# An attention and token-MLP block on one core: single-bank accumulator tiles, first norm transposed by DMA, three levels in the first MLP

## The chip, the cores and the metric

The kernel runs on one core of one Trainium2 chip. The metric is the device time of one execution in microseconds (us). The kernel before took 238.85 us (median of 4 runs made beside the changed kernel, 238.24 to 239.48). A ratio below is always the mean time of one kernel's fast runs over that of the other's fast runs of the same rounds on the same chip, so it is not quite the ratio of the medians that stand beside it. The medians and ranges of the experiments are over all runs. The span of a profiled execution, from first to last instruction, is about 2 us shorter than its time.

Engines are named as in the profile: PE is TensorE (matmuls), PEld its weight loads, DVE is VectorE, ACT is ScalarE, POOL is GpSimd, SP is SyncE, whose queue issues the DMAs.

## The reference, cut to what matters

```python
# S = 2048 tokens, D = 512, H = 32 heads of 16, window of 8 keys at distance 0, 2, ..., 14; F = 1792
x = A_x
sa, ca, ga, sb, cb, gb = the six rows of silu(c) @ w_mod          # "mod rows"
h = layernorm(x) * (1 + ca) + sa                                  # first norm
q, k, v = h @ wqkv
o = softmax over the 8 keys (q . k / 4, keys before the start masked) applied to v
x = x + ga * (o @ wo)
h = layernorm(x) * (1 + cb) + sb                                  # second norm
u = gelu(layernorm(h) mixed over TOKENS by w1 (S x F) + b1)       # third norm, first MLP
x = x + gb * (u mixed back over tokens by w2 (F x S) + b2)        # second MLP
```

Tokens are worked in 16 tiles of 128, grouped in five chunks of 2, 4, 4, 4 and 2 tiles. The attention of one chunk is: norm, transpose, QKV matmuls, products of query and key on VectorE (summed over a head by TensorE), softmax, products of weight and value on VectorE (summed by TensorE), output projection. The value products need shifted copies of v, called vD, which DMAs make inside the on-chip memory, 16 a chunk. The first MLP sums over all 2048 tokens, so it can begin on the tiles that are done and end only with the last one.

## The kernel before, cut to what the change touches

The program is a graph of operations with estimated durations. A small list scheduler in the kernel decides each engine's order of instructions once, from those estimates and from priorities; on the chip the order of each engine is fixed. Any change of a duration, a priority or a buffer count can therefore move instructions far away.

```python
psG = [psp.tile([P, 1024], F32, name=f"psG{i}") for i in range(3)]     # three accumulator tiles of two banks
def ps(slot):
    lo = slot.i % 2 * 512
    return psG[slot.i // 2][:, lo:lo + slot.size * 512]                # a slot is one bank or a pair
PR = dict(tr=1, qkv=2, a2=2, o=2, wo=2, mlp=2)                         # how many banks a group takes
w_raw_t = T([P, KT * 3 * D], BF, "w_raw")                              # q, k and v weights in one tile
# ... [cut]
# first norm of a chunk -> n_sb (one buffer); 16 transposes a chunk of four tiles on TensorE into an
# accumulator; scaled by (1 + ca), sa on the way out
for k2 in range(KG):
    for sl in tiles:
        nc.tensor.transpose(trp[:, ...], n_sb[:, sl, (k0 + k2) * P:(k0 + k2 + 1) * P], ident[:])
# ... [cut]
# first MLP in four levels of tiles: 0-5, 6-9, 10-13, 14-15. At the end of a level the partial sums are
# parked in gT (bf16); the next level carries them in again by a matmul with the identity.
LEVELS=(2, 3, 4)
nc.tensor.matmul(bank(), lhsT=ident[:], rhs=gT[:, ft, :], start=True, stop=False)   # carry-in, 14 a level
```

## Time and profile before

| | before |
|---|---|
| time, median | 238.85 us |
| span of the profiled run | 236.5 us |
| TensorE busy | 206.4 us (87%) |
| VectorE busy | 157.8 us (67%) |
| chunk 0's QKV begins | 10.55 us |
| chunk 1's QKV begins | 33.90 us |

First part of the page (busy us, share of the span, instructions), before:

```profile
PE 206.4 (87%) x1413; PEld 100.6 (43%) x1436; DVE 157.8 (67%) x231; ACT 129.4 (55%) x209; POOL 3.7 (2%) x29
```

Second part of the page, before: the span in 40 slices of 5.9 us, busy tenths of TensorE and its granted clock in tenths of full speed.

```profile
PE   0493678899988995889999999999999999999992
...
PEclk9999599999999999999999999999999999999998
```

TensorE is the fullest engine and is full from the middle on. Its idle time lies at the start and around the fifth to the eighteenth slice, where it works beside a nearly full VectorE. In the fifth slice the clock is halved too. In the first slices the clock row is no measure: it shows 9 there, yet equal groups of matmuls ran at very different speed (the timeline below); the trace's record of the clock begins only with its first change (at 16.7 us here).

The costliest groups of the page, before (busy us, mean ns of one, then the idle time before them and what ended it):

```profile
L188 PE MATMUL psG_63<-hT_71,w_raw 128*128 128x256 bf16 (+1 forms) x62 | 13.0, 360 | 3.3 <-DMA w_raw<-in_A_wqkv_dram 3.2
...
L188 DVE TENSOR_TENSOR big_78<-q_sb_72,k_c_74 128x2048 bf16<-128x2048 bf16 (+1 forms) x5 | 8.2, 1646 | 8.9 <-issue 8.9
```

Chunk 0's QKV waited 3.2 us for weights, and VectorE stood 8.9 us before its first query-key product.

The timeline of TensorE, before (start, duration, what; in brackets the wait before it):

```profile
10.55 0.37 PE L188 MATMUL psG_63<-hT_71,w_raw 128*128 128x256 bf16 x1 [2.20 <-DMA w_raw<-in_A_wqkv_dram]
11.96 3.39 PE L188 MATMUL psG_63<-hT_71,w_raw 128*128 128x256 bf16 x15 [1.04 <-DMA w_raw<-in_A_wqkv_dram]
15.14 2.67 PE L188 MATMUL psG_61<-hT_71,w_raw 128*128 128x256 bf16 x16
17.65 1.91 PE L188 MATMUL psG_62<-hT_71,w_raw 128*128 128x256 bf16 x16
...
33.90 1.89 PE L188 MATMUL psG_61<-hT_71,w_raw 128*128 128x512 bf16 x8 [0.49 <-DVE ga_bc L188]
```

Equal groups of 16 matmuls take 3.4, 2.7 and 1.9 us. The table of stretches, before (start:end, length, then busy us and instructions of each engine, granted clock, DMA share, GB/s):

```profile
40.00:60.00 20.00, 19.00 (x146) 9.00 (x147) 18.69 (x23) 13.45 (x22) 0.00 (x0) 1.00 0.65 141
60.00:80.00 20.00, 17.67 (x157) 8.31 (x159) 19.81 (x18) 17.63 (x27) 0.00 (x0) 1.00 0.83 118
80.00:100.00 20.00, 17.12 (x130) 9.53 (x131) 18.36 (x26) 16.09 (x32) 0.00 (x0) 1.00 0.35 63
100.00:120.00 20.00, 18.58 (x184) 8.91 (x186) 17.69 (x13) 14.16 (x23) 0.00 (x0) 1.00 0.75 164
...
33.90:232.30 198.40, 189.08 (x1273) 88.78 (x1294) 139.70 (x190) 115.21 (x185) 0.00 (x0) 1.00 0.53 124
```

The first column after the length is TensorE. From chunk 1's QKV to the last matmul it is busy 189.1 us of 198.4, so idle 9.3.

### The profile page before, as it was taken

How to read it: one execution, taken by the hardware profiler on the slowest of the kernel's cores; microseconds unless marked ns; L12 is line 12 of the kernel's file. 1: busy time of each engine (PE TensorE's matmuls, PEld its weight loads, DVE VectorE, ACT ScalarE, POOL GpSimd, SP SyncE). 2: the span in 40 equal slices, each digit the busy share in tenths (PEclk: the TensorE clock that was granted, in tenths of full speed). 3: DMA queues.
4: the chain of work that ended last, by engine and by line, in shares of the span. 5: the costliest groups of instructions: out<-in, count | busy, mean ns of one | idle time of the engine just before them, and what ended most of it. 6: DMA issues, size and time to landing. Idle time of an engine off the chain costs nothing.

```text
span 236.5 us, 3678 instructions
## 1 busy us (share of the span) xinstructions
PE 206.4 (87%) x1413; PEld 100.6 (43%) x1436; DVE 157.8 (67%) x231; ACT 129.4 (55%) x209; POOL 3.7 (2%) x29
## 2 busy tenths in 40 slices
PE   0493678899988995889999999999999999999992
PEld 0372434444443343653433334434444444444451
DVE  4207979997999979989969987662600044444445
ACT  3324649567997699695578688755769300000000
POOL 6000000000000000000000000000000000000000
PEclk9999599999999999999999999999999999999998
DMA  6999634359919930339954810479795511111411
GB/s 198 353 304 309 139 114 147 118 180 158 157 31 154 155 45 0 93 117 223 186 139 123 237 46 8 127 227 264 229 251 141 155 47 44 44 44 47 122 44 46
DMA packets 42565, 32.92 MB, mean 139 GB/s; under 512 B 4020, under 2 KB 42292, under 8 KB 42548
## 3 DMA queue, kind: packets, MB, share of 16 engines
q1 hardware_dynamic: 42540, 32.69, 56.1%
q8 instruction: 11, 0.18, 0.4%
q14 instruction: 6, 0.05, 0.1%
q10 hardware_dynamic: 8, 0.00, 0.0%
HBM read 22.03 MB, written 2.10 MB: 102 GB/s over the span
## 4 chain that ended last, share of the span: by engine, by line
PE 58%; DVE 17%; ACT 11%; issue 7%; DMA 4%; SPq 1%; DVEq 0%; ACTq 0%
PE psG_61 L188 21%; PE psG_62 L188 21%; PE psG_63 L188 15%; ACT xx L188 3%; DMA w_raw<-in_A_wqkv_dram 3%; DVE big_78 L188 2%; DVE big_79 L188 2%; DVE st_0_1_123 L188 2%; DVE big_80 L188 2%; ACT junk L188 2%; ACT h_69 L188 2%; PE psL L188 1%; DMA vD_93<-v_c_77 1%; SPq L188 1%; DVE st_2_1_143 L188 1%
## 5 line engine op out<-in xcount | busy, mean ns | idle before, releaser
L188 PEld LDWEIGHTS <-w_raw 128*128 128x128 bf16 x282 | 30.8, 114 | 28.1 <-issue 7.6
L188 DVE SCALAR_TENSOR_TENSOR o_sb_95<-psG_62,b2col,gb_bc 128x512 f32<-128x512 f32 x6 | 4.5, 748 | 24.6 <-PE psG_62 L188 24.6
L188 PEld LDWEIGHTS <-wst_99 128*128 128x128 bf16 x128 | 12.2, 98 | 15.6 <-issue 1.8
L188 PE MATMUL psG_61<-hT_71,w_raw 128*128 128x512 bf16 (+1 forms) x78 | 17.8, 372 | 0.9 <-DVE ga_bc L188 0.5
L188 PE MATMUL psG_62<-hT_71,w_raw 128*128 128x256 bf16 (+1 forms) x95 | 17.7, 327 | 0.5 <-ACT hT_71 L188 0.4
L188 PEld LDWEIGHTS <-wst_100 128*128 128x128 bf16 x128 | 12.4, 98 | 12.6 <-issue 0.8
L188 PE MATMUL psG_63<-hT_71,w_raw 128*128 128x256 bf16 (+1 forms) x62 | 13.0, 360 | 3.3 <-DMA w_raw<-in_A_wqkv_dram 3.2
L188 DVE TENSOR_TENSOR big_78<-q_sb_72,k_c_74 128x2048 bf16<-128x2048 bf16 (+1 forms) x5 | 8.2, 1646 | 8.9 <-issue 8.9
L188 PEld LDWEIGHTS <-ident 128*128 128x128 bf16 (+1 forms) x99 | 7.9, 97 | 12.4 <-issue 5.6
L188 PEld LDWEIGHTS <-wst_98 128*128 128x128 bf16 x80 | 7.5, 98 | 10.7 <-issue 2.9
L188 DVE TENSOR_TENSOR n_sb<-o_sb_95,xx 128x512 bf16<-128x512 f32 (+1 forms) x17 | 11.2, 660 | 0.6
L188 PE MATMUL psG_62<-h_69,wst_99 128*128 128x512 bf16 x40 | 10.8, 379 | 0.5 <-issue 0.3
L188 ACT ACTIVATE gT<-psG_62 128x1024 bf16<-128x1024 f32 x9 | 9.2, 1017 | 3.4 <-PE psG_62 L188 3.4
L188 PE MATMUL psG_63<-h_69,wst_99 128*128 128x512 bf16 x39 | 10.7, 380 | 0.1
L188 DVE SCALAR_TENSOR_TENSOR o_sb_95<-psG_61,b2col,gb_bc 128x512 f32<-128x512 f32 (+1 forms) x6 | 4.2, 703 | 8.0 <-PE psG_61 L188 8.0
L188 PEld LDWEIGHTS <-o_sb_95 128*128 128x128 bf16 x64 | 6.0, 98 | 7.9 <-issue 0.8
L188 DVE TENSOR_TENSOR big_80<-q_sb_73,k_c_75 128x4096 bf16<-128x4096 bf16 x4 | 9.1, 2282 | 0.0
L188 PE MATMUL psG_62<-h_69,wst_100 128*128 128x512 bf16 x35 | 8.9, 380 | 0.1
L188 ACT ACTIVATE gT<-psG_63 128x1024 bf16<-128x1024 f32 x7 | 7.1, 1016 | 2.7 <-PE psG_63 L188 2.7
L188 DVE BATCH_NORM_STATS2 st_1_0_132<-xx 128x6 f32<-128x512 bf16 x6 | 4.1, 675 | 6.6 <-ACT xx L188 6.6
L188 DVE SCALAR_TENSOR_TENSOR o_sb_95<-psG_63,b2col,gb_bc 128x512 f32<-128x512 f32 (+1 forms) x5 | 3.5, 693 | 6.3 <-PE psG_63 L188 6.3
L188 PEld LDWEIGHTS <-group_102 128*32 128x32 bf16 x128 | 2.7, 95 | 11.3 <-issue 10.5
(211 smaller groups left out, 427.8 us busy)
## 6 DMA issues: line engine op xcount, KB each, us to landing
wst_99<-in_B_w_dram SPq DMA_DIRECT2D x3, 768.0 KB, 5.2
wst_100<-in_B_w_dram SPq DMA_DIRECT2D x3, 768.0 KB, 4.7
out_dram<-n_sb SPq DMA_DIRECT2D x15, 128.0 KB, 1.7
wst_99<-in_B_w_dram SPq DMA_DIRECT2D x2, 896.0 KB, 4.9
w_raw<-in_A_wqkv_dram SPq DMA_DIRECT2D x3, 512.0 KB, 7.1
xx<-in_A_x_dram SPq DMA_DIRECT2D x3, 512.0 KB, 9.2
w_raw<-in_B_w_dram SPq DMA_DIRECT2D x1, 1344.0 KB, 8.1
vD_93<-v_c_77 SPq DMA_DIRECT2D x8, 130.0 KB, 3.6
```

The source lines that it names most:

```text
L188: r = fn(*a, **k)
```

## The change

The intent: take work from TensorE (fewer carry-ins, transposes done by DMA), start earlier (loads in the order in which they are needed, weights in three tiles so that nothing waits for all of them, warm-up matmuls), and let evictions and matmuls interleave more finely (one-bank tiles). The second norm's sums of nine tiles come from ScalarE's accumulated output; before it was six. The scheduler's priorities were tuned anew.

```diff
-    LEVELS=(2, 3, 4),
+    BOUNDS=(6, 10),            # three levels: tiles 0-5, 6-9, 10-15
+    NPRE=5,                    # five groups of the last level start before its last tiles are there
-    NHT: int = 1,
+    NHT: int = 2,
-    LN2A=(0, 2, 2, 2, 0),
+    POOLN1=(3, 5, 7, 8, 11),   # first norm of five tiles on GpSimd
+    LN2D=(2, 3, 10, 11, 12, 14, 15),   # second norm's sums on VectorE; the others on ScalarE
+    XDMA=(1, 2, 3, 4),         # chunks whose transposes are DMAs
...
-    psG = [psp.tile([P, 1024], F32, name=f"psG{i}") for i in range(3)]
+    psS = [psp.tile([P, 512], F32, name=f"psS{i}") for i in range(6)]
-    w_raw_t = T([P, KT * 3 * D], BF, "w_raw")
+    w_r = ring(3, [P, KT, D], BF, "w_qkv")
...
+    def f_warm():
+        for i in range(36):
+            nc.tensor.matmul(ps(s_w)[:, 0:P], lhsT=ident[:], rhs=ident[:], start=True, stop=True)
...
+    dma(rowA, wmod_view[:, :, 3 * D:6 * D], 3 * D * D * 2, [], ["rowA"], "ld_wmod345")   # 1.5 MB in one load
...
+        if ch in XDMA:
+            for sl, st in enumerate(tiles):
+                nc.sync.dma_start_transpose(out=hT[:, :, sl * P:(sl + 1) * P], in_=h3[:, st, :])
+            # then hT is scaled in place on ScalarE or VectorE
...
+RANK = {'st1': -69.27, 'ln1': -327.95, 'tr': -152.8, ...}     # priorities, tuned
+BIAS = {'n1': 1.63, 'hT': 2.81, 'ev': 1.88, ...}
```

Cut: the rewriting of the norms' helper functions for one tile at a time, the homes of the second MLP's weights, four output buffers instead of two. The first norm is now computed ahead into the buffer h3, where the third norm's results go later.

## The prediction

> **What bounds it now.** The span is 236.5 us (median time 238.9). Busy times: TensorE 206.4, VectorE 157.8, ScalarE 129.4. In the table of stretches TensorE is 87% full, and its idle time lies in three places: before 10.5 us (loads, first norm), 18–54 us (8.8 us idle; 6.8 us of it also at a granted clock of 0.5), 54–120 us (6.6 us idle). After 120 us it is idle under 1 us until 230.7; then 5.8 us of tail. So: start-up latency, then TensorE and VectorE coupled, then TensorE alone.
>
> In the timeline, chunk 0's first query-key product starts at 18.96 (VectorE idle 8.9 us): its 48 QKV matmuls start at 10.55, stall for a weight load and run slowly (first group 3.4, last 1.9). Chunk 1's QKV starts at 33.9.
>
> **What the change does to TensorE.**
> - Levels of the first MLP go from four to three: 14 carry-in matmuls fewer, at 0.216 us each (from the timeline: 1.29 per six): −3.0 us.
> - 56 of 64 transposes go to DMA: the transposes hold 6.0 us, so −5.0 us.
> - 36 dummy matmuls before the first load lands take the slow clock away from chunk 0's QKV: about −2.3 us. The Trainium skill ("TensorE: Matmul & The Clock Gate", Part 1) has the array at half clock until busy for some 3.4 us; the 3.4/2.7/1.9 us of equal QKV groups agree.
>
> **Start-up.** Weights in three tiles and the first query/key groups evicted by half banks let the first product start at about 13.5 instead of 19 (estimate: start 10.5, 32 matmuls of 256 columns at 0.11 us, partly). But the order puts chunk 1's hT scaling behind chunk 0's a2 eviction on ScalarE, and about 6 MB of loads stand before the first transposes in the queue (about 18 us at the 350 GB/s of the 6–12 us stretch). Estimate for chunk 1's QKV: about 28.5 instead of 33.9.
>
> **What stays.** VectorE's work hardly changes: counting its instructions with the trace's durations gives the same total (nine parks of 0.68 us come, norms leave). ScalarE rises by about 6 us (512-wide evictions at 0.58 against 1.02 for 1024). Five norms go to GpSimd, hidden.
>
> **Sum.** TensorE: 196.8 from 33.9 to 230.7, minus 8.5 idle, 3.0 carry-ins, 3.6 transposes, 2 mod rows: 179.5. 28.5 + 179.5 + 5.8 tail = 214 without idle. VectorE: 118 us of work after 24.5 us, thus last h3 at 142 without gaps; after it 73 matmuls (15.8), the second MLP (48.4) and the tail: 212. Both are nearly full, in fixed order, so I add 6 us of mutual waits: span about 219.
>
> **Predicted: 221 us**, range 214 to 229. Faster by over 2%: 0.95; within 2%: 0.04; slower: 0.01.
>
> **What would show it.** First query-key product at 13–15 us, chunk 1's QKV at 27–30, no slow clock in chunk 0's QKV; TensorE busy about 195; VectorE's busy time within 3 us of before, last h3 at 146–151; TensorE full from there; tail unchanged near 5.8 us.
>
> **What would make it wrong.** The trace has no DMA transposes. The skill ("DMA: Bandwidth & Descriptors", Latency and other measured facts) gives 261 GB/s for them, an estimated 0.5 us for 128 KB; if each takes several us or holds the queue in front of the vD copies, chunks 2 to 4 wait and TensorE idles (230 or more). A slow-clock stretch at 18–25 us may stay. If the order fits the chip better, waits fall to 2 us: 215.

## The result, and the profile after

| | before | after |
|---|---|---|
| time, median (lowest to highest) | 238.85 us (238.24 to 239.48) | 227.82 us (226.77 to 228.17) |
| ratio of fast runs (95% interval) | | 0.9529 (0.9497 to 0.9561) |
| span of the profiled run | 236.5 us | 225.9 us |
| first query-key product | 18.96 us | 15.33 us |
| chunk 1's QKV begins | 33.90 us | 35.54 us |
| from there to the end of the span | 202.6 us | 190.4 us |

The kernel became 4.7% faster. The last two rows say where: chunk 1's QKV begins 1.6 us later, and 12.2 us were won after it. The mark is not quite like for like. In the kernel before, two of the four mod rows, the end of chunk 0's softmax and its value sums come after chunk 1's QKV has begun; in the changed kernel all mod rows, the softmax and two of the four value sums come before it.

First and second part of the page, after (slices of 5.6 us):

```profile
PE 205.7 (91%) x1380; PEld 98.5 (44%) x1402; DVE 157.9 (70%) x236; ACT 131.2 (58%) x279; POOL 11.6 (5%) x35
...
PE   7596647879999999989999999999999999999993
...
PEclk9769885999999999999999999999999999999999
```

VectorE's busy time did not change (157.8 and 157.9). The dip of TensorE in the sixteenth slice (5 tenths before) is gone. The clock row is low in more of the first slices than before; since the row is no measure in the first slices (above), this does not show that TensorE was slower there than before.

The costliest groups of the page, after:

```profile
L191 PE MATMUL psS<-hT,w_qkv 128*128 128x512 bf16 (+1 forms) x235 | 50.2, 363 | 1.3 <-ACT hT L191 0.7
...
L191 DVE TENSOR_TENSOR big<-a2sb,vD 128x4096 bf16<-128x4096 bf16 (+1 forms) x20 | 36.9, 1860 | 6.9 <-DMA vD<-v_c 6.7
```

The QKV matmuls do not wait for weights any more. VectorE now waits 6.7 us for the vD copies.

The timeline of TensorE, after:

```profile
9.22 8.95 PE L191 MATMUL psS<-hT,w_qkv 128*128 128x256 bf16 x48 [0.65 <-ACT hT L191]
...
24.85 1.04 PE L191 MATMUL psS<-gT,sc_rep 128*128 128x512 bf16 x4 [0.95 <-DMA gT<-in_w_mod_dram]
25.72 0.40 PE L191 MATMUL psS<-lsb,ident 128*128 128x64 bf16 x8
25.95 3.57 PE L191 MATMUL psS<-gT,sc_rep 128*128 128x512 bf16 x8
...
29.59 0.42 PE L191 MATMUL psS<-lsb,selA 128*32 128x64 bf16 x32
32.80 0.62 PE L191 MATMUL psS<-big,stack 128*32 128x256 bf16 x8 [2.79 <-DVE big L191]
34.99 0.62 PE L191 MATMUL psS<-big,stack 128*32 128x256 bf16 x8 [1.57 <-DVE big L191]
35.54 1.90 PE L191 MATMUL psS<-hT,w_qkv 128*128 128x512 bf16 x4
```

In TensorE's order the mod rows' matmuls (`gT,sc_rep`), chunk 0's softmax (`lsb`) and two of its value sums (`big,stack`) all stand before chunk 1's QKV, the last line. What comes before them waits for a 1.5 MB load and for VectorE.

On ScalarE, after, the scaling of chunk 1's transposed input stands behind the eviction of chunk 0's softmax weights:

```profile
30.76 0.58 ACT L191 ACTIVATE a2sb<-psS 128x512 bf16<-128x512 f32 x1
...
32.41 2.93 ACT L191 ACTIVATE hT<-hT,sacol,a1col 128x512 bf16<-128x512 bf16 x4
```

The queue that issues the DMAs, after (timeline of SyncE):

```profile
21.59 5.13 SPq L191 DMA_DIRECT2D vD<-v_c  x6
26.82 3.86 SPq L191 DMA_TRANSPOSE hT<-h  x3
30.72 2.56 SPq L191 DMA_DIRECT2D vD<-v_c  x4
33.40 1.21 SPq L191 DMA_TRANSPOSE hT<-h  x1
34.65 4.09 SPq L191 DMA_DIRECT2D vD<-v_c  x5
38.84 3.85 SPq L191 DMA_TRANSPOSE hT<-h  x3
42.74 0.61 SPq L191 DMA_DIRECT2D vD<-v_c  x1
```

The queue is occupied almost without a gap from 21.6 to 42.7 us. In these lines one transpose of 128 KB holds it for 1.2 to 1.3 us, and a vD copy for 0.6 to 0.9 on average. The copies of chunk 0 and the transposes of chunks 1 and 2 take turns. The last copy of chunk 0 is issued at 42.74, behind three transposes of chunk 2. VectorE's last value product of chunk 0 waits for it, and TensorE's fourth value sum for that product (timelines of VectorE and of TensorE, after):

```profile
45.06 1.23 DVE L191 TENSOR_TENSOR big<-a2sb,vD 128x2048 bf16<-128x2048 bf16 x1 [2.49 <-DMA vD<-v_c]
```

```profile
46.34 0.40 PE L191 MATMUL psS<-big,stack 128*32 128x256 bf16 x8 [1.94 <-DVE big L191]
```

The table of stretches, after:

```profile
8.90:15.70 6.80, 6.23 (x28) 4.10 (x29) 3.52 (x9) 3.27 (x7) 0.00 (x0) 0.50 1.11 344
...
40.00:60.00 20.00, 17.85 (x120) 8.10 (x121) 16.60 (x14) 15.03 (x28) 0.00 (x0) 1.00 0.82 201
60.00:80.00 20.00, 19.39 (x189) 8.75 (x190) 19.15 (x16) 18.25 (x42) 0.00 (x0) 1.00 0.87 129
80.00:100.00 20.00, 18.95 (x139) 9.19 (x140) 19.07 (x23) 19.39 (x46) 0.00 (x0) 1.00 0.96 148
100.00:120.00 20.00, 19.84 (x157) 9.45 (x157) 19.66 (x29) 18.10 (x43) 0.00 (x0) 1.00 1.13 189
...
35.54:222.51 186.97, 182.26 (x1168) 83.54 (x1185) 134.54 (x185) 111.14 (x239) 0.00 (x0) 0.99 0.65 140
```

From chunk 1's QKV to the last matmul TensorE is busy 182.3 us (before 189.1) and idle 4.7 (before 9.3). So of the 11.4 us won there 6.8 are busy time and 4.6 are waits; the tail after the last matmul gives the other 0.8. The 6.8 us are not all removed work: two mod rows only moved in front of the mark, and from 35.5 to 39.6 us the changed kernel runs at half clock, where the kernel before did not. The largest wait that remains is between 40 and 60 us, 2.15 us, of which 1.94 is the wait just shown.

### The profile page after: what moved, and what is told of

Read it like the earlier page. It is cut to its first block, busy times and chain, and to the rows that moved or that the text cites. A ratio compares the mean times of both kernels' runs of the same rounds, so it can differ in the third digit from the quotient of the medians.

```text
span 225.9 us, 3720 instructions
## 1 busy us (share of the span) xinstructions
PE 205.7 (91%) x1380; PEld 98.5 (44%) x1402; DVE 157.9 (70%) x236; ACT 131.2 (58%) x279; POOL 11.6 (5%) x35
## 4 chain that ended last, share of the span: by engine, by line
PE 61%; DMA 12%; SPq 9%; ACT 8%; DVE 6%; issue 3%; DVEq 0%; ACTq 0%
PE psS L191 58%; SPq L191 9%; DMA gT<-in_w_mod_dram 5%; DVE big L191 5%; DMA vD<-v_c 5%; PE psL L191 2%; ACT hT L191 2%; DMA hT<-h 2%; ACT h L191 2%; ACT xx L191 1%; ACT junk L191 1%; ACT v_c L191 1%; ACT a2sb L191 1%; DVE m L191 1%; DVE st L191 1%
## 5 line engine op out<-in xcount | busy, mean ns | idle before, releaser
L191 PE MATMUL psS<-h,wst 128*128 128x512 bf16 x216 | 53.2, 379 | 0.4
L191 PE MATMUL psS<-hT,w_qkv 128*128 128x512 bf16 (+1 forms) x235 | 50.2, 363 | 1.3 <-ACT hT L191 0.7
L191 PEld LDWEIGHTS <-wst 128*128 128x128 bf16 x308 | 29.7, 98 | 33.1 <-issue 1.5
L191 PEld LDWEIGHTS <-w_qkv 128*128 128x128 bf16 x282 | 31.1, 116 | 27.8 <-issue 9.3
L191 DVE TENSOR_TENSOR big<-a2sb,vD 128x4096 bf16<-128x4096 bf16 (+1 forms) x20 | 36.9, 1860 | 6.9 <-DMA vD<-v_c 6.7
L191 DVE SCALAR_TENSOR_TENSOR h<-psS,bcol,gb_bc 128x512 f32<-128x512 f32 (+1 forms) x17 | 12.2, 719 | 41.3 <-PE psS L191 41.3
L191 DVE TENSOR_TENSOR big<-q_sb,k_c 128x4096 bf16<-128x4096 bf16 (+1 forms) x20 | 36.8, 1857 | 0.5 <-PE psL L191 0.5
L191 DVE BATCH_NORM_STATS2 st<-xx 128x6 f32<-128x512 bf16 x23 | 15.6, 677 | 7.9 <-DMA xx<-in_A_x_dram 7.2
L191 ACT ACTIVATE h<-xx,nb,rs 128x512 bf16<-128x512 bf16 x26 | 19.9, 804 | 0.2 <-DVE nb L191 0.2
L191 PE MATMUL psS<-gT,big 128*128 128x512 bf16 x82 | 18.2, 379 | 0.1
L191 PE MATMUL psS<-woq,o_sb 128*128 128x512 bf16 x60 | 16.3, 380 | 1.2 <-ACT o_sb L191 0.9
L191 PEld LDWEIGHTS <-big 128*128 128x128 bf16 x116 | 9.2, 97 | 11.4 <-DMA big<-in_w_mod_dram 1.2
```

What stands on the lines that cost most here:

```text
L191: r = fn(*a, **k)
```

## The experiments

Twelve kernels ran, each with five rounds beside the kernel before. The changed kernel is 0.9529, or 227.82 us, in the same measure. The questions were: which part of the change brings the gain after 35 us, and why did the start-up bring none? Where an expectation names a theory by a letter, C is the clock (TensorE too slow at the start), D the one-bank tiles as the source of the gain, and E the 1.5 MB load of the mod rows. Some edits leave the order of instructions as it was; others make the scheduler find a new order, and then the order is a second change. Each paragraph says which. Running the kernels' scheduler again confirms it: it gives the same list of operations wherever the text says "same order". It also corrects a name. What the expectations of the two runs with copies on GpSimd call the start of chunk 2's QKV (46.7 us) is the group after chunk 0's last value sum; by that list it is chunk 1's last query-key group, and chunk 2's QKV begins at 53.00 us.

### Transposes back on TensorE, for all chunks (new order)

```diff
-        ...prompt_kernel(tc, *args)
+        ...prompt_kernel(tc, *args, XDMA=())
```

> All 64 transposes go back to TensorE, everything else of the change kept (the scheduler orders anew). Theory A (the DMA transposes buy TensorE time, as predicted): TensorE's transposes come back, 56 x 0.09 us, and the time rises by about 5 us, to 233. Theory B (in the start-up they cost on the one DMA-issuing queue, 1.3 us of issue each, what they save on TensorE): chunk 1's QKV starts earlier than 35.5 us (30 to 32) and the total stays within 2 us of 227.8.

Measured: 230.33 us, ratio 0.9645 (0.9614 to 0.9676). In this new order the DMA transposes are worth about 2.5 us net (2.8 by the ratios), half of the 5.0 us of TensorE work that they remove by my estimate. The start differs more than the total. Timeline of TensorE in this kernel:

```profile
24.48 1.02 PE L191 MATMUL psS<-hT,w_qkv 128*128 128x512 bf16 x4
...
30.20 1.92 PE L191 MATMUL psS<-hT,w_qkv 128*128 128x512 bf16 x7
```

Chunk 1's QKV begins 11 us earlier, though only with its first four matmuls (the next begin at 30.20, in the changed kernel at 37.66), and the kernel is still slower. An early start of chunk 1 is not worth its own length when the order later loses it.

### Transposes back on TensorE for chunk 1 alone (new order)

```diff
+        ...prompt_kernel(tc, *args, XDMA=(2, 3, 4))
```

> Only chunk 1's four transposes go back to TensorE, which is idle at that time anyway; chunks 2 to 4 stay on DMA. Theory B: the vD copies of chunk 0 no longer stand behind 5 us of transpose issues, chunk 1's QKV starts at 30 to 32 instead of 35.5, total about 224. Theory A (start-up bound by the 1.5 MB modulation load and the slow clock, not by the issue queue): QKV start within 1 us of 35.5, total within 1.5 us of 227.8.

Measured: 229.27 us (227.44 to 233.82; two of the six runs slow), ratio 0.9576 (0.9547 to 0.9606). By the ratios that is 1.1 us slower than the changed kernel, but the intervals overlap, so it is not clear of noise; it is not faster, though chunk 1's QKV begins at 24.3 us (again with four matmuls; the next at 29.4). Here too the gain at the start was lost in the new order: between 60 and 120 us, most of it from 80 to 100, where TensorE is busy 15.28 us instead of 18.95. This miss shows that the start of chunk 1 alone does not set the total.

### Plain copies in place of the transposes (same order, result wrong)

```diff
-  nc.sync.dma_start_transpose(out=hT[:, :, sl * P:(sl + 1) * P], in_=h3[:, st, :])
+  nc.sync.dma_start(hT[:, :, sl * P:(sl + 1) * P], h3[:, st, :].rearrange("p (k n) -> p k n", k=KT))
```

> Every DMA transpose is replaced by a plain DMA copy of the same 128 KB from the same tile to the same place, in exactly the same order (wrong result on purpose). Theory B (issue cost of transposes on the queue delays the vD copies and hT): issues fall from 1.3 to about 0.5 us each, 14 x 0.8 = 11 us of queue time goes, of which the 8 in the first 45 us count: chunk 1's QKV starts at 31 to 33, total 224 to 225. Theory A: the time stays within 1 us.

Measured: 224.38 us (222.62 to 224.84), ratio 0.9374 (0.9345 to 0.9403); relative error 0.021, wrong. So with the same bytes, order and buffers, the kind of the DMA costs 3.4 us. From issue to landing the two kinds hardly differ (median of the eight up to 43 us: 2.6 us for a transpose, 2.4 for a copy). The timeline of SyncE in this kernel shows what differs:

```profile
26.17 2.00 SPq L191 DMA_DIRECT2D hT<-h  x3
...
35.15 2.76 SPq L191 DMA_DIRECT2D hT<-h  x3
```

Three issues take 2.00 and 2.76 us instead of 3.86 and 3.85. Chunk 0's last value sum no longer waits, and chunk 1's last query-key group begins at 44.18 us instead of 46.67 (chunk 2's QKV at 50.51 instead of 53.00). Chunk 1's QKV begins at 34.82 instead of 35.54. That is no more than between runs: with one warm-up matmul and the old queue (below) it is 34.81. So the queue is not what holds that one.

### Four levels in the first MLP again (new order)

```diff
+        ...prompt_kernel(tc, *args, BOUNDS=(6, 10, 14))
```

> First MLP in four levels as before (14 carry-in matmuls more, 14 parks more), the rest of the change kept, order scheduled anew. If TensorE bounds the second half one to one, 14 x 0.216 = 3.0 us more, 230 to 231. Rival: VectorE and ScalarE waits hide it, or the earlier start of level 10-14 gives it back: within 1 us.

Measured: 230.16 us (229.84 to 230.51), ratio 0.9635 (0.9615 to 0.9654). The 14 carry-ins are worth 2.3 us (2.5 by the ratios); I had 3.0 (14 times 0.216). The new order is TensorE's old one for its first 199 of 248 operations, so little else changed.

### One warm-up matmul instead of 36 (same order)

```diff
-        for i in range(36):
+        for i in range(1):
```

> 35 of the 36 dummy matmuls are taken away, all else in the same order. After's trace shows the granted clock full from 5.5 to 8.9 us, when TensorE only waits, and half from 8.9 to 15.7, when chunk 0's QKV runs (48 matmuls in 8.95 us, 7.6 before the change). Theory C (the dummies end too early, so they buy nothing): time within 1 us of 227.8, QKV block again 7.5 to 9 us. Rival, the prediction's: without them QKV is slower still and the total rises by about 2 us.

Measured: 228.44 us (226.29 to 230.27; three of the six runs slow, the fast ones 226.29 to 227.19), ratio 0.9499 (0.9461 to 0.9537): no difference clear of noise. Chunk 0's 48 QKV matmuls begin at 10.1 us and take 7.8, instead of 9.2 and 8.95, so they end at about the same time. TensorE is busy 3.6 us less, which answers one wrong point of the prediction: these matmuls count as busy time and do nothing else.

### Dummy matmuls in more of the gaps (same order)

```diff
+    def spin(slot, n):
+        for _ in range(n):
+            nc.tensor.matmul(ps(slot)[:, 0:P], lhsT=ident[:], rhs=ident[:], start=True, stop=True)
+    # 24 before the mod columns, 12 before chunk 0's transposes, 16 before its QKV,
+    # 14 and 24 before two of the mod rows, 44 before chunk 0's first value sum
```

> Dummy matmuls are put also into the idle gaps that follow (before the two modulation-column groups, before chunk 0's transposes and QKV, before two modulation rows, before chunk 0's first value product), all else in the same order. Theory C (slow clock at 9-16, 26-29 and 33-40 us is a real cost of the start-up): chunk 0's QKV takes 5.5 to 6 us instead of 8.95, no half clock before 40 us, total 222 to 225. Rival (start-up bound by loads, the issue queue and VectorE, TensorE's speed does not matter there): within 1 us of 227.8.

Measured: 232.0 us (229.95 to 233.74; one of the six runs slow), ratio 0.9698 (0.9655 to 0.974), 4 us slower. The clock was what I wanted in chunk 0's QKV. Timeline of TensorE in this kernel:

```profile
11.94 5.07 PE L191 MATMUL psS<-hT,w_qkv 128*128 128x256 bf16 x45 [0.19 <-ACT hT L191]
...
37.19 5.31 PE L191 MATMUL psS<-hT,w_qkv 128*128 128x512 bf16 x12
```

Chunk 0's QKV ran at full speed, 45 matmuls in 5.07 us, and chunk 1's began 1.7 us later than without the dummies. So a full clock in chunk 0's QKV alone does not bring an earlier start, and theory C's 222 to 225 us did not come. That the clock costs nothing is not shown: the run does not separate what the dummies themselves delay, and the issuing queue was slower in it too (the six vD copies took 6.05 us instead of 5.13, the three transposes after them 5.00 instead of 3.86), so that chunk 0's second value product waited 2.59 us for its copies instead of 0.89.

### The vD copies of chunks 0 and 1 issued by GpSimd (same order)

```diff
-        return add("sp", 0.6, lambda: nc.sync.dma_start(...
+        return add("sp", 0.6, lambda: getattr(nc, q).dma_start(...       # q="sync" unless given
-        f"vd{ch}_{dhi}{w4}", rate=150e3, ...)
+        f"vd{ch}_{dhi}{w4}", rate=150e3, q="gpsimd" if ch < 2 else "sync", ...)
```

> The 32 vD copies of chunks 0 and 1 are issued by GpSimd, which is nearly idle, instead of the queue that issues the transposes; order otherwise the same. Theory B (queue time of transposes and vD copies, one behind the other, holds chunk 0's value products and chunk 2's hT): vD waits of VectorE fall from 6.7 us to under 2, chunk 2's QKV starts 2 us or more before 46.7, total 224 to 225, as with plain copies. Rival: GpSimd's issue is as slow, or the landing and not the issue counts: within 1 us, or slower.

Measured: 229.45 us (228.05 to 232.8; one of the six runs slow), ratio 0.9604 (0.9551 to 0.9657), slower than the changed kernel by 1.6 us, just about clear of noise (the intervals touch). Chunk 1's last query-key group did begin 3.2 us earlier (43.51). It was lost between 60 and 80 us: chunk 1's copies landed after 8.1 us, ScalarE waited 4.9 us for transposes, and TensorE was busy 8.0 of the 10 us from 60 to 70.

### Only chunk 0's 16 vD copies issued by GpSimd (same order)

The same edit with `ch < 1`.

> Only chunk 0's 16 vD copies are issued by GpSimd; in vd_pool chunk 2's QKV began at 43.5 instead of 46.7 us, but chunk 1's copies, issued there too, then collided with chunk 3's transposes (8.1 us to land, ScalarE waited 4.9 us for hT). Theory B: the start-up gain of about 3 us stays now, total 224 to 226. Rival: the gain is given back anyway because VectorE and ScalarE set the pace after 50 us: within 1 us of 227.8.

Measured: 225.0 us (223.8 to 228.03; one of the six runs slow), ratio 0.9388 (0.9356 to 0.9419), and the result is correct. It beats both kernels: 2.8 us below the changed one, and 6.1% below the kernel before. The table of stretches of this kernel:

```profile
40.00:60.00 20.00, 20.00 (x128) 8.62 (x126) 17.43 (x14) 15.76 (x31) 0.00 (x0) 0.95 0.87 185
60.00:80.00 20.00, 19.79 (x198) 8.61 (x197) 19.03 (x19) 18.74 (x42) 0.00 (x0) 1.00 0.85 134
```

TensorE's remaining wait between 40 and 60 us is gone (20.00 busy instead of 17.85, a little of it at half clock). The DMAs did not land sooner after their issue: the vD copies took 6.6 us (median) instead of 3.1, the transposes up to 43 us 8.8 instead of 2.6. Together with the plain copies this shows that the occupied issuing queue cost the changed kernel about 3 us there. The Trainium skill ("DMA: Bandwidth & Descriptors", Rules for kernel authors) says of spreading DMAs over several engines that it does not help bandwidth, "it only saves sequencer issue time". Issue time was what was short, and 16 issues moved away brought 2.8 us. Chunk 1's QKV still began at 34.75 us.

### The six one-bank tiles declared as three two-bank tiles (same order)

```diff
-    psS = [psp.tile([P, 512], F32, name=f"psS{i}") for i in range(6)]
+    psG = [psp.tile([P, 1024], F32, name=f"psG{i}") for i in range(3)]
-        return psS[slot.i][:]
+        return psG[slot.i // 2][:, slot.i % 2 * 512:slot.i % 2 * 512 + 512]
```

> The six single-bank PSUM tiles are declared as three tiles of two banks again, still used bank by bank, in the same order; the built program then waits on later events of the neighbour bank. Theory D (single-bank tiles pay by finer waits): 2 to 5 us slower, as TensorE waits for evictions of the bank beside. Rival: the waits were slack anyway: within 1 us.

Measured: 240.2 us (239.01 to 240.81), ratio 1.0046 (1.0013 to 1.008). The same instructions in the same order, on the same bytes, are 12.4 us slower than the changed kernel: the whole gain and a little more. Only the declaration changed, so only the waits that are derived from it can differ. Two views of this kernel, first the table of stretches:

```profile
160.00:180.00 20.00, 18.45 (x85) 8.20 (x84) 5.38 (x12) 9.94 (x16) 0.00 (x0) 1.00 0.40 112
```

and the timeline of TensorE:

```profile
168.94 1.03 PE L191 MATMUL psG<-h,wst 128*128 128x512 bf16 x4
170.75 0.59 PE L191 MATMUL psG<-h,wst 128*128 128x512 bf16 x2 [0.78 <-ACT gT L191]
```

In the last level of the first MLP, where the changed kernel is busy 19.89 of 20 us, TensorE stops in the middle of a group of six matmuls, in a bank that it is already filling, until ScalarE has emptied another one. That this is the other bank of the pair is inferred from the declaration; the trace does not name the bank. This stretch shows 1.4 of the 12.4 us; most other stretches between 20 and 200 us lose 0.7 to 2.2 us each. The Trainium skill ("PSUM — Partial Sum Buffer", PSUM bank collisions raise a hardware error) gives the bank as the unit to guard: "Semaphore-guard PSUM by bank × quadrant (by bank is the simple version), not by address." A two-bank tile is guarded more coarsely than that. No run here shows a collision; what this one shows is the price of the coarser guard.

### The kernel before with six one-bank tiles (new order)

```diff
-    PR = dict(tr=1, qkv=2, a2=2, o=2, wo=2, mlp=2)
+    PR = dict(tr=1, qkv=1, a2=1, o=1, wo=1, mlp=1)
-    psG = [psp.tile([P, 1024], F32, name=f"psG{i}") for i in range(3)]
+    psS = [psp.tile([P, 512], F32, name=f"psS{i}") for i in range(6)]
```

> The kernel before, with one part of the change alone: six single-bank PSUM tiles in place of three two-bank tiles, so all evictions become one bank wide (the scheduler orders anew). Undoing that declaration in the changed kernel cost 12.4 us, more than the whole gain. Theory D (the two-bank tile couples neighbours, and freeing them is the main source of the gain, in whatever order): before gains 3 us or more, 236 or less. Rival D2 (the kernel before already claims and frees both banks of a pair together, so it suffered little from it; the 12 us are what the new order would lose without single-bank tiles): within 2 us of 238.8, or slower because 1024-wide evictions (1.02 us) become two of 0.58.

Measured: 237.82 us (236.38 to 238.94), ratio 0.9951 (0.9917 to 0.9984). Alone, one-bank tiles bring 1.2 us. The two runs belong together: the tiles are needed for the new order to work, and alone they do not bring the gain. One limit remains: the priorities were not tuned again for this kernel, so what a tuned order would make of the tiles alone is not shown.

### The mod-row load put later (new order)

```diff
-    dma(rowA, wmod_view[:, :, 3 * D:6 * D], ...)                        # among the first loads
+    dma(rowA, wmod_view[:, :, 3 * D:6 * D], ..., after=last vD of chunk 0)
```

The twelve matmuls of these rows and the first MLP's first weight loads moved behind it.

> The 1.5 MB load of three modulation rows, their 12 matmuls and the first MLP weight loads go behind chunk 0's vD copies; rows are needed only from about 70 us (scheduler orders anew; vD copies stay on the old queue). Theory E (chunk 0's softmax stood behind those matmuls on TensorE, from 24.0 to 29.5 us): first value product before 29 instead of 31.5 us, chunk 1's QKV at 31 to 33 instead of 35.5, total 224 to 226. Rival: the queue of DMA issues holds chunk 1's QKV at 35 anyway: within 1 us of 227.8.

Measured: 232.74 us (232.33 to 233.86), ratio 0.9745 (0.9716 to 0.9773), 5 us slower. Chunk 1's QKV begins at 33.78, only 1.8 us earlier, and chunk 2's is then 0.8 us later than in the changed kernel (53.84 instead of 53.00). Later, between 100 and 120 us, TensorE loses time (busy 17.71 us instead of 19.84). In this order theory E explains 1.8 us; what the load costs in the old order was not tried.

### The second norm's sums of all tiles on VectorE (new order)

```diff
+        ...prompt_kernel(tc, *args, LN2D=tuple(range(16)))
```

> The changed kernel with the second norm's sums of all tiles on VectorE, as bn_stats, instead of some on ScalarE through accumulated sums; the list schedule is made anew. Theory: this adds about nine times 0.61 + 0.18 us of VectorE work, some 7 us, at a stage (55 to 110 us) where VectorE is nearly full: 1.5 to 4 us slower than the changed kernel (229.5 to 232 us, ratio to the kernel before 0.959 to 0.970). Rival: TensorE has its work there in any case, and ScalarE is freed by as much; within 1 us of the changed kernel (ratio 0.949 to 0.957).

Measured: 243.77 us (242.31 to 244.89), ratio 1.0197 (1.0161 to 1.0233). That is 16 us slower, far outside what both theories expected. The work itself was as expected. VectorE's norm statistics in the stretch from 50 to 110 us, in the changed kernel and then in this one:

```profile
50.00:110.00 60.00, 7.37 (x18) 1.00 0.95 151
```

```profile
50.00:110.00 60.00, 13.97 (x34) 1.00 1.05 144
```

That is 6.6 us more. But the scheduler answered with another order: chunk 4's last value product ends at 156.9 us instead of 136.7, and the third norm of the last tiles ends at 170.4 instead of 158.1. Timeline of TensorE in this kernel:

```profile
153.46 0.40 PE L191 MATMUL psS<-big,stack 128*32 128x256 bf16 x8 [3.50 <-DVE big L191]
...
170.13 4.43 PE L191 MATMUL psS<-h,wst 128*128 128x512 bf16 x10 [5.10 <-DVE h L191]
```

TensorE stands 3.5 and 5.1 us because the last tiles come late. Up to 140 us nothing is lost: from 40 to 140 us TensorE is busy 96.0 us here and 95.9 in the changed kernel, and between 140 and 180 us 9.2 us less. That points to the order, not to the stage where the work was added. How much of the 16 us is the added work and how much is the new order is left open; it takes a version with the old order. It moves nine tiles, and the change itself moved three.

## Why the prediction was right or wrong

The total was predicted at 221 us with 214 to 229, and measured at 227.8: inside the range, 7 us above the point. Almost all of the 7 us is one term.

**The failed step** is the prediction's "Estimate for chunk 1's QKV: about 28.5 instead of 33.9." It began at 35.5, 7.0 us later than estimated. The rest of the sum held: from chunk 1's QKV to the end of the span I had 219 minus 28.5, that is 190.5 us, and measured were 190.4 (225.9 minus 35.5). That it fits so exactly is partly luck. In the prediction's own terms, with a tail that begins at the last 14 matmuls, TensorE's work was 180.8 us (predicted 179.5), its waits 4.7 (6) and the tail 4.9 (5.8): misses of about 1 us that cancel.

What the runs showed in its place:

- The step before it was nearly right. The first query-key product began at 15.33 us (predicted 13 to 15; before 18.96). These 3.6 us were spent before chunk 1's QKV.
- The prediction named the cause itself, the scaling of chunk 1's input behind chunk 0's softmax eviction on ScalarE, and underestimated it. That eviction began at 30.76 us, and the scaling took until 35.3. What it had not put in front of the eviction is in the timeline: the 1.5 MB load, issued at 12.74, landed at 24.80; then eight of the twelve mod-row matmuls took 3.57 us at half clock, and only then, at 29.59, came the last sums of chunk 0's softmax. TensorE's order has a second chain of the same length: two value sums, the second of which starts at 34.99. The prediction did not split its 28.5 into terms, so the 7 us cannot be divided among these.
- Making the queue faster moves this start by 0.7 to 0.8 us (34.82 with plain copies, 34.75 with the copies on GpSimd), no more than the run with one warm-up matmul (34.81). A faster clock for chunk 0, with dummies, does not bring it forward (37.19). Moving the mod rows gives 1.8 us (33.78), in another order. Transposes on TensorE do move it (24.48), in another order, and the total gets worse. So the two chains hold it together, in the fixed order: in the changed kernel the value sum ends last (TensorE waits 1.57 us for it), in the run with chunk 0's copies on GpSimd the scaling does (0.33 us, after the first matmul). Which of them would be the last if both were shortened was not tried and stays open.
- What would have happened with a start at 28.5 is open too. The two runs in which chunk 1 began at 24 us were not faster, so the 7 us cannot be said to be simply there for the taking.

**The warm-up term** (2.3 us) was wrong. I expected no slow clock in chunk 0's QKV, and it ran in the slow clock from 8.9 to 15.7 us (the stretch with 0.50). In the 3.4 us before, when the clock was full, TensorE was busy for 1.62 us. The Trainium skill ("TensorE: Matmul & The Clock Gate", Part 1) describes the activity window as free-running and 3.4 us long, and the slow stretches here, 6.8, 3.4 and 6.8 us, agree with multiples of it. What I missed is that 36 short matmuls did not keep the clock up through these 3.4 us, though no single wait in them was longer than 0.9 us. One dummy matmul did as well as 36. The slow stretch that the prediction allowed for at 18 to 25 us came later, at 26.0 to 29.4 and 32.8 to 39.6.

**The queue** was among the things that "would make the prediction wrong", with the right place (in front of the vD copies) and a size of about 3 us: 3.4 by plain copies, 2.8 by moving 16 copies. My 0.5 us for a transpose was an estimate of the bytes; the queue's own 1.2 to 1.3 us to issue one is what counted.

**Point by point, the rest.**

- VectorE's busy time within 3 us of before: right (157.8 and 157.9).
- TensorE busy about 195: wrong (205.7). The 36 dummies are 3.6 us of it. Busy time also grew where the clock was halved, since a matmul then takes longer (eight mod-row matmuls 3.57 us, and 1.89 in the run with more dummies, where the clock was full); how much in all was not separated. The busy time of TensorE is no measure of its work when the clock differs.
- Last third norm at 146 to 151: wrong (158.1), late with the rest.
- TensorE full from there: right (19.89 of 20 us).
- Tail unchanged near 5.8: about 1 us shorter (4.9).
- ScalarE up by about 6 us: wrong (129.4 to 131.2). Five norms on GpSimd, hidden: not tested; the first two took 5.57 us, where the kernel's scheduler counts 0.9 for one.
- Work off TensorE after chunk 1's start: 8.6 us in the sum (3.0 carry-ins, 3.6 transposes, 2 mod rows), measured 6.8 of busy time. Of the busy time after, 3.84 us ran at half clock; at full clock it would be about 1.9 us less, by my estimate, and the difference about 8.7. Carry-ins alone: 3.0 predicted, 2.3 by experiment. Transposes: 3.6 to 5.0 predicted, 2.5 net by experiment, in a new order.
- Waits in the steady part: 6 us predicted for TensorE, 4.7 measured; before it was 9.3.

What the prediction did not see is how the gain hangs together. It treated the one-bank tiles as a detail; undone alone, they take away 12.4 us, and done alone, without new tuning, they bring 1.2.

## What to carry to other kernels

When the order of instructions is fixed, an estimate of a start-up has to follow every engine's order to the point that is asked for, and include the operations of the earlier stage that stand in front; the durations of the new stage alone come out too short. A DMA has a price in the queue that issues it besides its bytes: where many small DMAs stand in one queue, move some of them to an idle engine's queue, and measure, since moving twice as many lost the gain again here. Declare accumulator tiles no larger than the unit that is filled and emptied, and judge such a precondition by undoing it in the new kernel as well as by adding it to the old one.

## What the Trainium skill lacked or had wrong

- "Advanced Engine Details and Errata", X-Bar Transpose (TRN2), says "TRN2 transpose DMAs are as fast as regular DMAs". For 128 KB from on-chip memory to on-chip memory that is nearly so in time to landing (2.6 and 2.4 us) but not in the issuing queue: 1.22 us a transpose and 0.62 us a plain copy of the same tile to the same place (medians of 14), which made the kernel 3.4 us slower. No page gives such an issue time in microseconds for this size.
- "PSUM — Partial Sum Buffer" lacks that a tile declared over two banks can be made to wait as a whole: 12.4 us in this kernel, with the same instructions in the same order.
- "TensorE: Matmul & The Clock Gate" does not say how busy TensorE must be to keep the full clock. Here 3.4 us in which it was busy for 1.62 us, without a wait above 0.9 us, were followed by half clock, and the 36 warm-up matmuls before them bought nothing (ratios 0.9529 with 36, 0.9499 with 1).
- "SBUF — State Buffer", Who interferes with whom, has it right that a VectorE instruction with two inputs contends with a GpSimd instruction that reads. What it lacks is a size for this pair: two norms of 128x512 on GpSimd took 5.57 us beside VectorE's products at 17.8 us, and 1.53 us at 28.6 us. That the products are the cause was not tested.
